# Attention and two MLPs from one written order: a new order table, with 185 copies, conversions and additions on other engines

## The chip, the cores and the metric

The kernel runs on one core of a Trainium2 chip. The metric is the device time of one execution in microseconds; the median of three executions of the kernel before is 849.13 us (848.77 to 849.22).

## The reference

Windowed attention (4 batches, 8 heads, 576 positions, 64 per head; heads 0 to 3 look back over 32 positions, heads 4 to 7 over 32 positions that lie four apart) and behind it two MLPs with 2304 tokens, 512 model columns and 2048 hidden columns:

```python
scores = np.where(masks[None], scale * np.matmul(q, k.transpose(0, 1, 3, 2)), -1e9)
attn = np.exp(scores - np.max(scores, axis=-1, keepdims=True))
attn = attn / (np.sum(attn, axis=-1, keepdims=True) + 1e-09)
x = np.matmul(attn, v)                        # heads side by side: 2304 x 512
h = x @ moe_w_in;  r = np.maximum(h, 0.0);  x = (r * r) @ moe_w_out
h = x @ moe2_w_in; return (h * (1.0 / (1.0 + np.exp(-h)))) @ moe2_w_out
```

## The kernel before, in words

**Tiling.** The attention goes by half a batch (`h` = 0 to 7) and pair of heads (`pair` = 0 to 3), in units of 96 or 72 queries: scores on TensorE (L533), mask and minimum on VectorE (L558), exponential on ScalarE (L566, or L729 behind a transposition for the first eight blocks), the sum and its reciprocal on VectorE (L573, L575, L744, L746), normalisation (L586, L590, L592, L754), transposition (L602, L713) and the product with V (L625, L738). The first MLP takes its first three tiles of 256 tokens while the attention still runs (`mlp`, L788 to L790 and L836 to L838) and its last three tiles of 512 tokens by a product that saves one multiplication in eight (`mlp2`, L936 and L990 to L992). The second MLP takes three tiles of 768 tokens in the same saving form for both of its products (`strassen`, L1094 and L1179).

**Number format.** Every operand of a large product is split in a high part (a conversion, L245 on ScalarE, L247 on VectorE, L249 on GpSimd) and a low part (a subtraction, L252 on VectorE or GpSimd), and each product is three matmuls. The weights come as 64-bit numbers and are turned into such pairs by nine small operations (`weights`, L274 to L330); later tiles read the pairs, and sums of them, back from HBM (`stream`, L445, and `stream2`, L472).

**What sets the order.** Nothing is scheduled while the kernel is built. Each operation has a number, and the table `ORDER` (from line 1359) lists all 3960 of them with the engine that does each: P is TensorE, A is ScalarE, V is VectorE, G is GpSimd, D is a DMA. `@` gives the place of its buffers or banks. Every engine does its words in the table's order and waits, at the head of its queue, for what the word needs. All DMAs, loads and stores alike, stand in one queue, that of SyncE: a word that waits for its buffer holds all DMAs behind it. A load can start once the operation that last read its place is done. `F14` is not an operation of the program but 14 matmuls on zeros (`filler`, L1245), put where TensorE would otherwise sit still.

```python
            o.eng = {"P": "PE", "A": "ACT", "V": "DVE", "G": "Pool", "D": "DMA"}[word[0]]
...
            elif o.eng == "Pool":
                o.turn = turn
```

The second of these places makes a GpSimd operation wait for the last VectorE operation before it in the table that is marked with `lock`.

**Words that the prediction names.** `D2`, `D33`, `D64` and `D95` load Q and K of pairs 0 to 3 of the first half (L495), `D3`, `D34`, `D65` and `D96` their V; `P5`, `P36` and `P67` are the scores of pairs 0 to 2 (L533), `P10` the first transposition (L713), `P13` the first product with V (L738). `D126` and `D135` load the first weights (L274), `A136` is the first step of their conversion (L282). `A3958` is a one-column exponential that stands first on ScalarE (L1304). `D3196` loads a pair of weight sums for the second product of the second MLP (L472), `P3438` is the product that reads it (L1179); `D758`, `D998` and `D1091` load blocks of later halves (L486), and `P759`, `P999` and `P1092` are their scores.

Of the kernel before, what the change touches and what calls it, by code (L numbers as in the profile page):

```python
# [1363 lines left out]
V110 D152@56 P86@2 V76 V103 A137 V77 V112 P104@1 A78@8 V113 V87 F7@3 V97 V114 V88 A105 V130 D177@88 A89 P115@1
V139 P106@0 A116 V131 F1@2 P90@3 D169@80 P117@2 V140 A91@60 A93@64 A132@68 F5@1 V94 V92 A141@164 V107 V118
P400@3@1@72@0 V108 V119 D211@124 G133 A153@14 V109@12 V120 A162 V403 F2@2 V401 A145 P121@0 G142 V402 V410
D506@201 P404@2 V411 A122 A144@10 V123 V412 A154 V146 P1238@3 D186@92 V399 A161@2 V147 A170@0 V148 P413@1 A124
A405 V178@4 D220@128 A149@84 V125 V163 A1239@16 P406@0 V150 A414 A1240 V164 P415@2 A179 D194@108 V407 V155
P1244@3 A1241@6 V408 V165 A409@8 V416 V156 A166@100 D424@196 P507@0@1@96@1 V417 V1242 A418 V157 P1243 A1245@18
V167 A158@168 D151 V172 A1246 V510 A187@10 D134 P419@3 V159 P1250@2 A422@104 A420 V512 A1247@12 G189 V508 V423  # L1370
A513 V421 A171 D203@116 V1248 P426@3@0@112@2 V180 A1251@16 V173 A511 P1249 A509 V427 G174 V523 A1252 V428 A188
V429 V436 V438 A1253@14 P430@2 V525 A524 V437 V514 V521 A526 V515 V425 V1254 A522 P439@1 V190 A431 A516 V527
A517 V175@172 P432@3 V528 V176 A440 A529 P518@0 V530 A222 P441@2 V433 V181 A204@2 P531@1 P1255 V434 V442 A520
V182 A435@8 V443 V519 A533 V444 D539@196 A532 A183@120 V191 P534@3 A195@6 V184 P445@0 A537@12 A535 V446 P1256@1
A192@176 G197 V448 V536 A196 V447 D450@201 V449 V198 A205 V193 A1257@18 P540@0@3@20@3 A1258 V199 A1259@4 D237@40
A212@0 V1260 V554 A200@28 P1261 V556 G206 V545 A557 V558 V543 A555 D254@76 V541 V201 A559 P452@0@3@24@0 A542
V560 V207 A544 A546 V561 D538 V451 P1262@1 V208 D271@112 A562 A563 V547 V465 V548 V455 A549 V466 G550 V454
P564@2 V463 A1263@16 D228@36 V464 A565 V456 A1264 V453 A566 V209@180 P551@1 A1265@8 V214 P457@2 A552 A553 V210
A221@14 D245@72 P567@1 V215 A458 A213 V223 P467@0 V1266 A238@12 V216 P459@3 A568 A468 V224 D572@196 A570@4
A217@32 P469@2 V240 A229@10 V225 P1267 A256 V460 V470 V461 V471 G218 V462@6 A239 D478@201 V472 A246@8 V569  # L1380
P473@0 V231 P1274@1 A476@52 A474 V241 A230 V475 A226@184 D262@92 V477 V232 P573@3@0@56@1 A1275@18 V227 A1276
A1277@2 V233 D296@116 A255@6 P480@1@2@80@2 V589 V587 A234@88 G1278 V580 V593 V576 A590 V574 G235 V591 P1279 A247
V483 D305@24 V484 V482 A592 V481 V493 A575 V492 V494 A581 P485@0 V578 V491 A577 D202 V248 A588 V263@10 P495@3
A579 V242 A486 A594 V582 P1286@0 A243@188 V583 D279@108 V479 V595 V584 A272@0 V596 V249 P585@1 V597 A1287@16
P487@2 D219 V244 A586 A496 P598@1 V250 A1288 D571 P497@3 D288@124 A599 V488 A1289@2 V489 P600@0 A490@14 V498
V1290 V499 V251@96 P1291 V257 A500 V252 D605@201 A603@4 V265 P501@2 V258 P1298@1 A504 A502 V601 A280@8 D638@196
V503 V505 V274 P1268@3 V602 A1299@18 V275 A1300 D322@56 A264 V259 P606@2@1@20@3 A273 V266 A1301@12 P1280@0
A1269@16 D604 V611 G281 D313@80 V609 V626 A1270 V620 V624 A610 V607 V267 A625 P1292@3 A1271@2 V613 A260@192 V622
V1302 A290 V261 P1304@2 A1281@18 V282 A612 V1272 A621 V268@128 A1293@16 V276 P639@1@36@0 A1294 A614 V269 A623
P640@3 A627 A1282 V628 V641 P1273 A608 V645 A1283@14 V615 V652 V629 G1284 V616 V654 A630 V643 V656 P1303 V289@2  # L1390
# [12 lines left out]
P1358@2 A722 A328@140 V1350 V1575@14 P1364@3 V1356 A1359@16 V329 D1573 A1360 A331@4 V1576@24 V1578@84 P1370@2
A1361@0 V1577 A1365@18 V1569 D693 A1366 A1580 D356@108 V1362 P727@3@80@3 V1579 A1371@16 V343 A1583 P1351 A1372
V733 D1570 V731 V729 V735 V344 A736 P723@2 A734 V1584 A345@148 P728@3 V333 A730 V1581 A1367@10 P1357 A732 V1368
A724@6 V742 D758@196 A332 V746 V737 V748 V744 V357@14 P1382@2 A745 V738 A749 V739 D1585 A743 V334 A747 P740@3
A1383@18 V358 P1363 A741 V335 A1373@2 D364@36 A1384 V750 A336@116 V751 V359 P759@3@2@76@0 V1374 A1385@8 V337
A752 D321 P1369 V773 V762 D725 V760 A348@0 V775 V764 D1582 A761 V1386 P1376@3 V350 A763 V349 A765 V777 A774 V766
# [265 lines left out]
```

## Time and profile before

| | before |
|---|---|
| median of three executions | 849.13 us |
| the profiled execution, whole | 849.5 us |
| its span, first to last instruction | 847.7 us |
[...]
| TensorE busy | 839.2 us (99%) |
| VectorE busy | 638.8 us (75%) |
| ScalarE busy | 501.5 us (59%) |
| GpSimd busy | 122.2 us (14%) |
| moved by DMA | 223.56 MB |

The span is one execution from its first instruction to its last; 1.8 us of the execution's time lie outside it. The shares are means over the whole span, and the stages differ much: ScalarE and VectorE have most of their work in the first 200 us. TensorE's busy time holds the 53 filler matmuls too.

### The profile page before, as it was taken

To read this page: it belongs to the slowest core of one execution; us is meant where nothing else is said; L and a number is where in the kernel's file an instruction comes from. 1 tells how busy PE (TensorE), PEld (TensorE's weight loads), DVE (VectorE), ACT (ScalarE), POOL (GpSimd) and SP (SyncE) were. 2 spreads that over 40 slices of the span, in tenths; PEclk is the share of its full clock that TensorE was granted. 3 is DMA by queue.
4 is the path that set the end of the run, shared out by engine and by line. 5 is a ranking of instruction groups with operands and counts; after the bars stand their busy time and mean duration, and the time that the engine had idled before them with its cause. 6 is when DMAs were issued, how large, how long until landed. Compare 5 with 4: busy or idle time off the path is not lost.

```text
span 847.7 us, 16967 instructions
## 1 busy us (share of the span) xinstructions
PE 839.2 (99%) x6009; PEld 795.6 (94%) x6009; DVE 638.8 (75%) x1706; ACT 501.5 (59%) x1324; POOL 122.2 (14%) x142
## 2 busy tenths in 40 slices
PE   9989999999999999999999999999999999999998
PEld 7879999999989889889998999999999999999998
DVE  6999999888888698768899997578722488422765
ACT  5999988887666265334542566565445555345652
POOL 2220000101210202131201002102201111202020
PEclk9999999999999999999999999999999999999999
DMA  9585568879898888988999989889774774773441
GB/s 344 178 284 207 152 204 304 278 265 333 310 303 318 308 292 282 326 311 288 336 344 299 343 308 351 301 287 324 248 259 149 246 266 164 269 262 111 174 159 65
DMA packets 83603, 223.56 MB, mean 264 GB/s; under 512 B 8768, under 2 KB 18240, under 8 KB 83520
## 3 DMA queue, kind: packets, MB, share of 16 engines
q1 hardware_dynamic: 83520, 222.49, 75.2%
q8 instruction: 47, 0.77, 0.3%
q14 instruction: 36, 0.29, 0.1%
HBM read 172.13 MB, written 50.33 MB: 262 GB/s over the span
## 4 chain that ended last, share of the span: by engine, by line
PE 94%; ACT 3%; DVE 1%; issue 0%; POOL 0%; POOLq 0%; ACTq 0%
PE y L1094 17%; PE sa L1179 15%; PE s L936 15%; PE y L1179 6%; PE y L990 5%; PE y L991 5%; PE y L992 5%; PE sa L1094 4%; PE s L788 3%; PE s L789 2%; PE s L790 2%; PE ax L533 2%; PE y L836 2%; PE ax L625 2%; PE y L837 2%; PE y L838 2%
## 5 line engine op out<-in xcount | busy, mean ns | idle before, releaser
L245 ACT CAST hl<-gq 128x384 fp32r<-128x384 f32 x168 | 79.5, 513 | 58.7 <-PE sa L1179 28.6
L1094 PE MATMUL y<-xs,ws 128*128 128x384 f32 x552 | 107.5, 334 | 0.0
L252 DVE TENSOR_TENSOR hl<-gq,hl 128x384 fp32r<-128x384 f32 x144 | 78.9, 581 | 27.3 <-ACT hl L245 24.0
L1094 PEld LDWEIGHTS y<-xs,ws 128*128 128x128 f32 x552 | 96.6, 188 | 0.1
L1065 DVE TENSOR_TENSOR gq<-y,gq 128x384 f32<-128x384 f32 x46 | 25.0, 554 | 94.1 <-PE y L1094 82.9
L1070 ACT COPY gq<-y 128x384 f32<-128x384 f32 x92 | 42.7, 479 | 75.0 <-PE y L1094 67.6
L1179 PE MATMUL sa<-hl,wp 128*128 128x384 f32 x432 | 79.1, 334 | 0.0
L936 PE MATMUL s<-x,ws 128*128 128x256 f32 x576 | 76.2, 284 | 0.0
L990 PE MATMUL y<-g,w 128*128 128x512 f32 x192 | 76.2, 397 | 0.0
L1179 PEld LDWEIGHTS sa<-hl,wp 128*128 128x128 f32 x432 | 75.2, 188 | 0.0
L991 PE MATMUL y<-g,w 128*128 128x512 f32 x192 | 75.2, 392 | 0.0
L992 PE MATMUL y<-g,w 128*128 128x512 f32 x192 | 74.9, 390 | 0.0
L952 DVE TENSOR_TENSOR h<-s,h 128x512 f32<-128x512 f32 x96 | 59.4, 619 | 19.8 <-PE s L936 16.6
L936 PEld LDWEIGHTS s<-x,ws 128*128 128x128 f32 x576 | 72.2, 191 | 1.2
L245 ACT CAST g<-r 128x256 fp32r<-128x256 f32 (+1 forms) x86 | 42.9, 504 | 51.2 <-DVE r L972 42.8
L566 ACT ACTIVATE ap<-ap,ast 96x128 f32<-96x128 f32 (+3 forms) x168 | 62.2, 371 | 8.3 <-DVE ast L575 4.2
L788 PE MATMUL s<-x,w 128*128 128x256 f32 x192 | 56.4, 294 | 0.1
L790 PE MATMUL s<-x,w 128*128 128x256 f32 x192 | 54.3, 283 | 0.0
L789 PE MATMUL s<-x,w 128*128 128x256 f32 x192 | 54.2, 282 | 0.0
L1179 PE MATMUL y<-hl,sw 128*128 128x384 f32 x288 | 51.4, 334 | 0.0
L1179 PE MATMUL sa<-hl,sw 128*128 128x384 f32 x288 | 50.9, 334 | 0.0
L1179 PEld LDWEIGHTS y<-hl,sw 128*128 128x128 f32 x288 | 50.0, 188 | 0.0
(176 smaller groups left out, 2071.2 us busy)
## 6 DMA issues: line engine op xcount, KB each, us to landing
raw<-w SPq DMA_DIRECT2D x64, 512.0 KB, 6.3
ws<-w1x SPq DMA_DIRECT2D x48, 512.0 KB, 6.7
ws<-w2x SPq DMA_DIRECT2D x48, 512.0 KB, 5.4
sw<-w2y SPq DMA_DIRECT2D x48, 512.0 KB, 4.5
wa<-w1s SPq DMA_DIRECT2D x24, 512.0 KB, 6.8
wa<-w2s SPq DMA_DIRECT2D x24, 512.0 KB, 5.7
w1x<-st SPq DMA_DIRECT2D x16, 512.0 KB, 4.8
w2x<-st SPq DMA_DIRECT2D x16, 512.0 KB, 5.1
```

The source lines that it names most:

```text
L245: self.nc.scalar.copy(out=out, in_=in_)
L252: self.eng[eng].tensor_tensor(out=out, in0=a, in1=b, op=ALU.subtract)
L566: es.append(self.op({"ACT": c_act(nk) + 0.185}, lambda e, i=i, n=n, c=c, p=p, st=st: nc.scalar.activation(out=p.tile[:n, c], in_=p.tile[:n ...
L788: nc.tensor.matmul(o, wh.tile[:, s], xh, start=(kk == 0), stop=False)
L789: nc.tensor.matmul(o, wh.tile[:, s], xl, start=False, stop=False)
L790: nc.tensor.matmul(o, wl.tile[:, s], xh, start=False, stop=(kk == KC - 1))
L936: nc.tensor.matmul(bank.tile[:, o:o + 256], wp, xp, start=i == 0, stop=last, skip_group_check=True)
L990: nc.tensor.matmul(o, wh.tile[:, s], gh.tile, start=c == 0, stop=False)
L991: nc.tensor.matmul(o, wh.tile[:, s], gl.tile, start=False, stop=False)
L992: nc.tensor.matmul(o, wl.tile[:, s], gh.tile, start=False, stop=(c == NF - 1))
L1094: nc.tensor.matmul(o, w[part == 2].tile[:, kk * P:kk * P + P], x[b][part == 1].tile[:, kk * half:kk * half + half], start=new and not kk a ...
L1179: nc.tensor.matmul(o, u.tile[:, c * P:c * P + P], v.tile, start=new and not q and not part, stop=q == nf - 1 and part == 2, skip_group_che ...
```

## The change

Only `ORDER` changes. The operations, their arithmetic and the code that makes them are the same. Counted from the two tables:

- 185 operations change their engine: 81 from ScalarE to VectorE, 47 from VectorE to ScalarE, 47 from GpSimd to VectorE, 10 from GpSimd to ScalarE. VectorE has 1560 words in place of 1479, ScalarE 1068 in place of 1092, GpSimd 66 in place of 123. TensorE has the same 750 and SyncE the same 516.
- By TensorE's place in the table before: in the first 24 us 3 go from ScalarE to VectorE and 1 from GpSimd to VectorE (the two subtractions of `V20`, L691). To 64 us 3 go from ScalarE to VectorE and 4 back. From 64 to 190 us 32 go from ScalarE to VectorE, 15 back, 3 from GpSimd to VectorE and 1 from GpSimd to ScalarE. The other 123 lie behind 190 us: among them 43 from GpSimd to VectorE.
- The fillers are 47 matmuls in eight groups (10, 16, 2, 7, 4, 2, 3, 3) in place of 53 in nine.
- The first loads are in another order: before `D3 D2 D33 D64 D126 D34 D135 D65 D95 D96`, after `D2 D33 D64 D135 D95 D96 D3 D65 D34 D126`. `P36` stands ahead of the second group of fillers, not behind it.
- `A3958` stands behind 19 other words of ScalarE, the first of which is `A136`.
- Other transfers change their turn and their buffers. Counted in words of TensorE between the one that frees the place (or holds the queue) and the one that reads the load: `D3196` has 4 in place of 8, `D758`, `D998` and `D1091` have 4 in place of 5. The load of weight sums next in shortness, `D3592`, has 5 in place of 22. No other load that TensorE reads directly, behind the first 30 us, comes below 6 us by the durations of TensorE's words before.

```diff
 ORDER = """
-V1 A3958 G0 F14@0 D3@140 D2@132 D33@136 V4 D64@144 D126@24 P5@20@0 F15@2 V8 V7 D34@148 V6 V18 D135@32 V9 V19
-P10@3 P36@28@1 V17 V50 P67@36@2 G20 A12 V38 A11 V49 V37 D65@156 V48 P13@0 V39 V68 V40 D95@152 P21@1 F3@3 V51 A22
...
-V3416 P3409 V3420 A3433@119 D3195@100 A3389 G3434 P3413 A3436@131 V3137 D3196@96 P3417 G3431 P3421 A3442@128
...
+V1 F10@3 D2@146 P5@44@0 G0 V7 V19 V8 V17 V6 D33@172 P36@163@1 V9 V18 V37 V50 V49 V39 V48 V20 V38 V40 D64@11
+F16@3 D135@201 V51 A136@32 V138 V137 P10@3 A11 D95@20 A12 D96@131 V97 D3@100 D65@55 V4 P67@40@2 V79 V80 V68 V82
+V70 V71 P21@3 A22 A23 P41@2 A43 P52@0 A53 V81 D34@89 V35 A42 D126@176 P13@1 V14 V15 V69 V66 A54 P24@3 V25 V72
...
+V3468 A3469@3 V3476 V3446 V3428 V3498 V3480 V3504 D3197@186 V3456 D3194@104 P3426 D3195@99 P3429 P3432 D3196@120
+P3435 P3438 P3441 A3457@128 V3458 A3461@58 V3454 V3536 D3132@16 P3444 P3447 D3133 D3198@22 A3423 A3509@74
...
 """
```

## Rows read from the trace of the kernel before

**Rows 1.** The page, part 1: busy time, share and instructions of each engine.
```profile
span 847.7 us, 16967 instructions
PE 839.2 (99%) x6009; PEld 795.6 (94%) x6009; DVE 638.8 (75%) x1706; ACT 501.5 (59%) x1324; POOL 122.2 (14%) x142
```

**Rows 2.** Busy time by stretch: length, then PE, PEld, DVE, ACT, POOL, clock, DMA.
```profile
0.00:21.00 21.00, 19.43 (x199) 15.76 (x200) 13.24 (x93) 11.08 (x41) 4.95 (x15) 1.00 0.92 343
21.00:63.00 42.00, 38.65 (x388) 34.64 (x387) 41.09 (x179) 41.26 (x123) 9.06 (x11) 1.00 0.68 231
63.00:191.00 128.00, 127.86 (x1214) 122.50 (x1213) 119.26 (x406) 112.39 (x372) 5.40 (x8) 1.00 0.69 235
191.00:480.00 289.00, 289.00 (x2133) 261.33 (x2132) 243.00 (x615) 143.19 (x409) 48.35 (x61) 1.00 0.90 314
480.00:848.00 368.00, 364.22 (x2084) 361.33 (x2082) 222.16 (x418) 193.61 (x384) 54.40 (x48) 1.00 0.67 233
```

**Rows 3.** Waits of PE over the whole span: total, times, longest, in us.
```profile
PE y L837 <- POOL g L252: 0.9, 1, 0.9
PE y L836 <- ACT g L245: 0.8, 1, 0.8
PE ax L738 <- DVE x L252: 0.5, 1, 0.5
```

**Rows 4.** Timeline of the first 12 us: start, length, instruction, idle time before it.
```profile
0.72 1.28 ACT L1304 ACT_TABLE_LOAD   x1 [0.72 <-PEq L1665]
...
0.98 3.17 PE L1245 MATMUL fill<-warm 128*128 128x256 bf16 x14 [0.98 <-DVE warm L1237]
...
4.09 1.49 PE L533 MATMUL y<-w 64*96 64x96 f32 x12
...
5.51 2.52 PE L1245 MATMUL fill<-warm 128*128 128x256 bf16 x15
5.72 0.29 DVE L558 CUSTOM_DVE_ANT_0 ap<-y,mask 96x128 f32<-96x128 f32 x1 [2.39 <-PE y L533]
...
9.11 0.29 DVE L558 CUSTOM_DVE_ANT_0 ap<-y,mask 96x128 f32<-96x128 f32 x1 [1.60 <-PE y L533]
```

**Rows 5.** Groups of instructions: one conversion on ACT and on DVE.
```profile
L245 ACT CAST w<-cv 128x512 fp32r<-128x512 f32 x27 | 16.6, 619 | 0.7 <-DVE cv L318 0.7
...
L247 DVE CAST w<-cv 128x512 fp32r<-128x512 f32 x5 | 2.1, 414 | 0.0
```

**Rows 6.** Timeline near 800 us: DVE alone, DVE in a row, DVE beside POOL.
```profile
800.08 0.55 DVE L252 TENSOR_TENSOR gq<-gq 128x384 f32<-128x384 f32 x1
800.55 1.49 DVE L252 TENSOR_TENSOR hl<-gq,hl 128x384 fp32r<-128x384 f32 x3
...
803.63 2.71 DVE L252 TENSOR_TENSOR hl<-gq,hl 128x384 fp32r<-128x384 f32 x3 [0.66 <-ACT hl L245]
...
804.65 1.26 POOL L252 TENSOR_TENSOR gq<-gq 128x384 f32<-128x384 f32 x1 [0.49 <-DVE hl L252]
```

**Rows 7.** Waits of DVE between 63 and 191 us: the three longest, all on ACT.
```profile
DVE ast L573 <- ACT ap L566: 1.9, 7, 0.5
DVE g L252 <- ACT g L245: 1.3, 4, 0.4
DVE st L252 <- ACT st L245: 1.2, 2, 0.7
```

**Rows 8.** The chain, one group of six matmuls of the second MLP.
```profile
523.85 1.04 PE sa L1179 x6
```

**Rows 9.** DMA issues: count, KB each, median us from issue to landing.
```profile
sw<-w2y SPq DMA_DIRECT2D x48, 512.0 KB, 4.5
...
blk<-qkv SPq DMA_DIRECT2D x6, 544.0 KB, 3.7
...
blk<-qkv SPq DMA_DIRECT2D x6, 480.0 KB, 4.3
```

**Rows 10.** All loads of the weight sums (tile sw).
```profile
DMA to landing us min/median/max: 3.5/4.5/9.9
```

More of the change, by code (lines that the diff above doesn't have):

```diff
@@ L1364 @@
[L1364 to L1378, printed above, removed]
@@ L1404 @@
[L1404 to L1408, printed above, removed]
@@ new lines @@
+V26 P44@2 V83 V45 V46 P98@77@3 V110 A16@25 A27 D398@196 D177@121 A47@171 P55@0 P73@3 A74 P28@1 V100 V101 F2@2
+V56 V113 V57 V99 V58 P59@2 A29@44 A60 P84@3 A85 V102 V112 V30 P75@0 V31@48 A62 G127@169 G129 A128 V103 P104@3
+A105 A3958 V32 V76 V63 V61 P86@2 V77 V111 V114 A78@163 F7@1 V87 V88 A89 F4@1 P115@0 A116 V139 V130 P90@3 A93@64
+A91@60 V140 V131 A132@68 G133 A141@164 D152@158 D186@185 D143@8 A145 G142 P106@0 V107 V92 V94 V108 P117@2 V118
+V109@25 D160@101 D506@115 V119 V120 A153@98 P400@3@1@79@0 V403 F2@0 V411 V410 P121@0 F3@2 V412 V402 V401 A124
@@ new lines @@
+A331@155 V320 V333 P1346@2 A1347@80 A1348 D356@108 A1568 V1576@24 V326 V327 P1339 A1571 A720 P708@2 A709 P691@3
+A692@0 P1345 V1569 A340@9 V342 A1355@13 V343 V344 P721@3 A1349@157 A722 A328@140 P1358@2 A1359@151 A1360
+A1361@76 P1364@3 A1365@21 A1366 A1367@162 V332 V1356 V334 V1350 D236 V1577 V1368 P1370@2 A1371@3 A1372 A1373@160
+D726@201 V1578@84 V1572 P727@3@80@2 V731 V1579 A1583 V735 A736 V729 A732 V733 A734 V1362 V1584 P1351 P728@3
+V1374 P723@2 V748 A749 V329 D168 D693 V744 D347@112 D321 D1570 D758@196 D1573 P1357 A730 A724@15 D725 A745 V742
@@ new lines @@
+P937@3@2@56@2 D1711@30 D2132@128 V942 V953 A954 V2165 P1525 A1544@10 A1542@46 V951 V940 A941 V957 V955 A958
+V1546@120 V1548@13 A943 A952 A956 A1538@3 P2166 V938 V959 V960 A939 P2174@2 A2178@16 V944 A945 D1543
+P968@0@1@68@3 V986 V971 A972 A1704 G1705 V973 V961 P2167 V969 V975 V946 V947 A948 P2168 P2169 P962@3 V963 V1706
+V982 A974 P2175@2 V2179 G1699 V1700 P949@0 D2129@38 D935 P2176@3 A950 P964@2 D1539 D2130@96 D998@201 A983 A970
+V988 V984 D1701 A976 V977 V978 G979 A987 V1713 A985 V2180 V2181 A989 V1707 A1708@43 P2177@1 V990 V2182 V991
@@ new lines @@
+D2135@70 D2138@8 P2211@1 V2216 V1728 V2217@98 D1091@196 D1719 P1092@2@0@68@3 V1095 V1112 A1087 V1097 V1108 V1106
+P1088@3 A1089@128 V1110 V1099 V2221@47 V1093 D2141@0 D2145@56 D2139@38 D2151@130 D1028 D2144@23 D1059 D2142@32
+D1739@92 D2148@64 P2225@1 P2226@3 A1113 A1100 P2227@0 P2228@2 A1107 A1111 A2218@17 A2229@8 V2219 V2230 V2231
+P2220 V2232 A2222@51 V2223 A1094 V2233 P2224 A1098 A1096 V1101 V2238@21 A1109 V1114 V1102 A1103 D1090 D2146@80
+P1104@0 A1105 P2242@2 V1115 V1116 V1741 A2246@96 P1117@1 A1118 D2149@37 D1729 D2150@116 D2152@16 P2243@3 V1740@2
@@ new lines @@
+V2457 P2445 D2357@20 D2530@56 P2482@0 P2483@2 A2473@60 G1826 A1825 A2484@40 V2320@110 V2474 P2458 V2485
+A2321@104 V2322 A1871@6 V1872 D2531@18 D2533@64 D1822 G1873 A2324@36 V2486 V1827 V1828 V1874 V1875 A2477@196
+V2478 A1829@108 A1811 V1832@32 V2325 P2462 P2475 P2562@1 G1834@128 V1833 G1835 V2487 V2488 V2489@202 A2312@52
+A2310@76 A2318@112 V2493@81 A2494@88 V2311 V2313 V1830 A2490@10 A1839 V2319 D2532@116 P2563@2 P2564@3 D1878@124
+A1880 V1879@84 V1881 V1882 A1836 V1837 A2566@20 V2567 P2479 V2568 V1883 V2495 V2569 V1886@124 V2491 V1840
@@ new lines @@
+D3154@39 D3067 P3107 P3111 V3118 A2726@55 V3122 V3028 V3094 V2730 D3065 P3202 V2722 A2724@15 P3115 P3119
+D3156@35 P3204 P3206@0 V2725 V2727 G2731 A3203@52 P3208 A3205@61 A3209 P3123 P3210 A2732@28 V2733 V3211
+D3160@125 D3158@104 P3212 D3029 D3169@42 D3166@130 D3162@48 D3171@40 D3175@12 D3164@99 P3214 A3215@71 P3127
+P3216 P3219@3 D3183@180 V3217 A3213@68 V3220 P3221 P3223 A3222 A3218 D3163@4 P3226 V3227 A3224 V3207 A3225 P3228
+A3229@81 P3230 P3232 V3233 P3235@0 P3237 P3239 A3231@84 A3238 A3240 D3176@64 D3165@35 P3242 D3168@120 D3093
@@ new lines @@
+V3482 V3520 P3483 P3490@1@2 P3493 P3496 P3499 P3502 P3505 V3507 P3508 A3521@126 A3517@96 V3518 V3448 G3526
+D3568@100 V3137 V3138 D3565@14 V3540 A3139@55 A3541@47 V3484 A3529@51 V3486 D3485 D3561@132 D3487 D3555@4
+D3569@72 A3141@87 V3522 P3511 P3600 V3512 D3581@2 D3556@80 D3554@10 P3519 P3523 V3140 V3143 V3142 V3530 V3542
+A3144@34 V3148 V3145 A3146@74 V3151 A3149@40 V3150 V3147 V3514 P3527 P3531 P3535 P3539 D3573@119 D3576@174
+D3558@150 D3562@122 D3451 P3543 P3547 A3548@127 P3602 A3550 A3601@16 A3603@19 P3604@1 A3152@46 D3559@95 P3606
@@ new lines @@
+A3664 D3574@8 P3674 P3676 P3678 P3681@3 A3648 V3673 A3675@151 P3683 A3671 V3679 V3762 A3677@161 A3684 P3685
+A3686 P3688 V3689 D3578@12 D3582@127 D3579@96 P3690 P3692 P3694 V3695 V3682 V3666 A3737@114 A3691@68 A3693@71
+V3738 P3697@1 P3699 P3701 A3763@65 A3702 P3704 A3731@131 D3580@100 P3706 P3708 A3700 D3577@0 A3703 A3687
+A3707@22 V3732 V3753 A3754@119 P3710 V3766 V3755 V3698 V3711 P3713@0 P3715 P3717 G3729 P3730@1@2 A3743@124
+A3740@86 G3741 A3680 G3770 A3709@25 A3716 A3767@9 V3792 V3764 A3718 V3744 A3696 V3774 A3775@128 V3796 A3797@13
@@ new lines @@
+A3817@120 A3843@123 V3896 V3832 V3794 P3781 P3785 D3591@186 D3588@89 P3791 P3795 D3589@132 P3799 D3590@96
+A3889@101 A3786@126 A3787 V3835 V3844 V3854 V3866 A3809@4 V3838 A3855@176 A3892@90 V3887 V3814 V3810 V3899 V3856
+V3818 P3803 P3807 P3811 P3815 V3862 A3863@74 P3819 D3592@12 D3593@104 V3823 P3824 P3827 V3890 V3870 V3878 V3850
+A3851@119 V3864 V3914 D3595@86 D3594@130 P3830 A3867@65 A3840@41 V3852 V3893 V3841 V3918 A3904@187 V3905
+A3907@45 V3908 D3596@4 A3915@116 A3859@36 P3833 P3836 P3839 P3842 V3902 V3922 V3874 V3930 A3931@129 V3868 P3845
@@ new lines @@
+A3820@32 A3871@12 A3821 A3919@105 V3860 V3942 D3597@48 V3920 V3872 G3938 D3598@133 P3853 P3857 P3861 P3865 P3869
+P3873 A3943@5 A3939@113 A3879@8 V3848 V3880 V3932 A3923@19 A3875@87 V3876 V3924 D3599@41 P3877 P3881 V3846 V3934
+V3882 V3916 V3884 D3885 V3940 P3888@0@3 P3891 P3894 P3897 V3926 P3900 P3903 P3906 P3909 D3847 P3917 P3921
+A3927@48 V3910 V3928 P3925 P3929 P3933 V3944 A3935@174 V3936 P3937 P3941 P3945 P3948 A3946@81 P3949 P3950 V3912
+P3951 P3952 P3953 D3911 P3954 P3955 D3883 D3947 D3913 D3849 A3956 D3957
```

418 lines of the change are left out of this document (193 added, 225 removed).

## The prediction, made before the change was run

> **What bounds the kernel now.** I read the page's busy times first, then busy time by stretch, then TensorE's waits, then the first 12 us of the timeline.
>
> The page says that TensorE is busy for 839.2 of 847.7 us [rows 1]. So all that another order can win back is the rest, 8.5 us, and the fillers among the busy time. The stretches say where the rest lies [rows 2]: 1.57 us in the first 21 us, 3.35 us from 21 to 63 us, 0.14 us from 63 to 191, nothing from 191 to 480, and 3.78 us behind 480. The last is mainly the end: the final copy and store, which both tables have alike. So only the first 63 us hold a gain, about 4.9 us of idle time plus the fillers. Two groups of fillers there, of 14 and 15, take 3.17 and 2.52 us [rows 4]; they stand where TensorE has nothing to do, so taking a filler out wins nothing by itself.
>
> From 21 to 63 us VectorE is busy for 41.09 of 42 us (97.8%) and ScalarE for 41.26: both are full, and TensorE's waits there are for them, 0.5 to 0.9 us each [rows 2, 3]. From 63 to 191 us VectorE is busy for 119.26 of 128 us and ScalarE for 112.39, while TensorE hardly waits. That is the reserve of the stage: 8.7 us on VectorE, 15.6 us on ScalarE. Behind 191 us VectorE and ScalarE have room (46 us in the next 289, 146 in the last 368).
>
> **The change part by part.** *The start.* The scores of the first pair begin at 4.09 us, and VectorE's first minimum at 5.72 us, behind a wait of 2.39 us; at 9.11 us it waits 1.60 us more, for the second pair's scores, which stand behind the 15 fillers and the first transposition [rows 4]. After the change the Q and K of the pairs are loaded first, without V of pair 0 ahead of them, and `P36` stands ahead of its fillers. Ten fillers in place of 14, at 3.17/14 = 0.23 us each, end 0.9 us earlier, at 3.2 us. I put the gain at 0.7 us, because the Q and K block still has to land, plus the 1.60 us of the second wait: 2.3 us. Against it stand four operations more on VectorE before 24 us: three at 0.34 us (below) and the two subtractions of `V20`, about 0.5 us together, 1.5 us in all. V of pair 0 comes seventh and not first; `P13` waits for it, and what then runs in its place is the next pairs' work. Net: 0.8 us won. Bounds: 2.3 us won if the added work lies in VectorE's other waits, and 1.3 us lost (the table load below).
>
> *21 to 63 us.* Three operations go to VectorE and four leave it: nothing.
>
> *63 to 191 us.* Net 32 + 3 - 15 = 20 operations come to VectorE. A conversion takes 0.414 us there and 0.619 us on ScalarE [rows 5]. Neighbours on VectorE overlap: three of 0.55 us in a row take 1.49 us, so each but the first costs 0.47, 0.08 us less [rows 6]. At 0.414 - 0.07 = 0.344 us, 20 of them add 6.9 us: 119.3 + 6.9 = 126.2 us of work on VectorE in a stage of 128 us. ScalarE gives up 16 net, at 0.5 to 0.6 us some 8 us, and then has over 20 us of room. This trade is the centre of the change: it unloads the engine that has the larger reserve. If VectorE can be kept as full as it is from 21 to 63 us, 97.8%, the stage takes 126.2/0.978 = 129.0 us: 1.0 us lost. Bounds: nothing lost, if its remaining waits fit into 1.8 us; 6.9 us lost, if all 8.7 us of its idle time come again. I take 1.0, because the three longest of those waits, 4.4 us together, are for ScalarE [rows 7], and ScalarE is what gets lighter.
>
> [...] Beside one GpSimd addition of 1.26 us, three VectorE instructions took 2.71 us, where three alone took 1.49 [rows 6]: 1.2 us lost on VectorE. [...]
>
> *Behind 191 us.* 43 GpSimd operations go to VectorE, 0.5 us each, some 20 us; 46 and 146 us of room cover them, and TensorE stood still nowhere there. If that cover were gone in one place, the price is one late operand, 0.5 to 0.9 us as in [rows 3].
>
> *The transfers.* All stand in one queue, so I counted for every load how many words of TensorE lie between its release and its use. `D3196` falls from eight groups to four, of 1.04 us each [rows 8]: 4.2 us, where loads of its kind need 3.5 at least, 4.5 in the median and 9.9 at most [rows 10]. That makes 0.3 us of waiting, bounds nothing and 5.7 us. `D3592` has five groups, 5.2 us. `D758`, `D998` and `D1091` keep 4.8 to 4.9 us where their kinds land in 4.3 and 3.7 us [rows 9]: nothing, up to 1 us each if another load is ahead. I take 0.3 us for all.
>
> *The table load.* It runs now at 0.72 us, beside the first fillers, for 1.28 us [rows 4]. With `A3958` moved behind `A136`, it may run only ahead of the first exponential of the attention, at about 8 us; price 0 to 1.28 us, taken as 0, because V of pair 0, now late, holds `P13` at that time anyway. [...]
>
> **Sum:** -0.8 + 0 + 1.0 + 0 + 0.3 = +0.5 us. The profiled execution took 849.5 us, 0.4 us above the median of the three; from it 850.0, and against the median 849.6 us. A measurement of this kernel can tell about 0.2% (1.7 us) from no change, so I forecast **no difference that can be measured**.
>
> **The rivals.** *VectorE becomes the bound (slower).* Place: 63 to 191 us. What speaks for it: 126.2 us of work in 128 us, in an engine that takes its words strictly in order; and from 21 to 63 us, where VectorE and ScalarE are both full, TensorE lost 3.35 of 42 us [rows 2]. Against it: ScalarE is light then. If all 8.7 us of idle time come again, the stage takes 6.9 us more: 849.1 - 0.8 + 6.9 + 0.3 = 855.5 us. The forecast allows 2.8 us of idle time (129.0 - 126.2); slower by over 0.2% begins where 1.2 us more, some 4 us, come again.
>
> *The start wins more (faster).* VectorE begins 2.3 us earlier, the added work fits into waits, and the middle loses nothing since GpSimd holds VectorE up less: 849.1 - 2.3 = 846.8 us. For it: the two waits of 4.0 us together [rows 4] are real and their causes are moved. Against it: from 21 to 63 us both other engines stay full, so what is gained early has to pass through them.
>
> *The table load comes late (slower).* 1.28 us on ScalarE's first chain: 849.6 + 1.3 = 850.9 us, on the edge of what can be told.
>
> *The change doesn't do what it says:* it can't be, the table is the program's only order.
>
> **How the numbers follow.** No measurable difference 0.44, with its own range of 847.6 to 850.8 us; VectorE as the bound 0.34; a faster start 0.17; the late table load 0.05, which I count as slower. So faster 0.17, same 0.44, slower 0.39. The range runs from 847.0 us (half of the faster case) to 854.0 us (most of the slower one, up to some 5.4 us of loss in the middle).
>
> **What would show it.** Right: VectorE's first minimum near 5 us and no wait of 1.6 us near 9; VectorE busy for 97 to 98% from 63 to 191 us, ScalarE below 83%; TensorE's idle time there 0.5 to 2 us; no wait of TensorE on a DMA above 0.5 us but ahead of `P3438`. Wrong: VectorE below 95% with TensorE waiting on it (the slower rival), TensorE's idle time in the first 63 us below 3 us (the faster one), a table load between 7 and 10 us, or a wait on a load of over 1 us, which would mean that the count of words between release and use is no measure of a load's margin.

## The result, and the profile after

The change makes the kernel slower: 859.12 us in the median (857.05 to 859.43) against 849.08 us, a ratio of 1.0114 with a 95% interval of 1.0096 to 1.0131. The forecast was no difference that can be measured, 849.6 us, in a range of 847.0 to 854.0 us. Neither the forecast nor the slower rival (855.5 us) reached so far.

Part 1 of the page of the changed kernel, against [rows 1]:

```profile
span 857.5 us, 16888 instructions
PE 840.7 (98%) x6003; PEld 797.2 (93%) x6003; DVE 671.8 (78%) x1788; ACT 486.8 (57%) x1295; POOL 75.8 (9%) x79
```

Its busy times by the stretches of [rows 2] (columns: stretch, length, busy time of PE, PEld, DVE, ACT and POOL with the instructions, granted clock as a share of full speed, DMA share, GB/s):

```profile
0.00:21.00 21.00, 17.63 (x189) 14.25 (x189) 15.26 (x99) 11.28 (x40) 2.96 (x12) 1.00 0.91 335
21.00:63.00 42.00, 39.12 (x396) 35.30 (x397) 41.16 (x178) 40.23 (x122) 9.76 (x11) 1.00 0.76 258
63.00:191.00 128.00, 127.69 (x1214) 122.70 (x1213) 124.75 (x425) 105.14 (x350) 2.27 (x3) 1.00 0.67 224
191.00:480.00 289.00, 283.08 (x2073) 256.37 (x2073) 242.01 (x628) 132.94 (x394) 30.93 (x32) 0.99 0.84 299
480.00:857.50 377.50, 373.14 (x2136) 368.62 (x2135) 248.66 (x464) 197.24 (x393) 29.88 (x22) 1.00 0.67 240
```

The stage from 63 to 191 us is close to the forecast: VectorE is busy for 124.75 of 128 us (97.5%), ScalarE for 82%, and TensorE is idle for 0.31 us, under the 0.5 to 2 us that the prediction names. The new hole is in the row below it. Before, TensorE had no idle time from 191 to 480 us [rows 2]; now it has 5.9 us, and the mean clock is 0.99 (over the whole span 0.996 of full speed, 0.999 before).

To put the loss in place I matched TensorE's words in the two traces and added up how much longer each now takes until the next one begins (fillers are counted too; the stretches are those of the changed kernel):

```
0 to 21 us     -0.50       375 to 390 us  +1.39
21 to 63       -0.22       390 to 540     +0.27
63 to 192.6    +0.04       540 to 570     +0.67
192.6 to 215   +7.28       570 to the end +0.02
215 to 375     +0.19       sum            +9.14
```

The last 0.7 us of the two spans' difference (9.8 us) lies behind TensorE's last instruction, in the final copy and store. So the first 63 us win 0.7 us, the middle costs nothing, and 7.3 of the 10 us are lost in one place of some 20 us. The waits of TensorE behind 191 us name what it waited for there:

```profile
engine line waited for: us in total, times, longest us
PE y L836 <- DVE yo L247: 3.2, 1, 3.2
PE s L936 <- DMA ws<-w1x: 1.3, 1, 1.3
PE y L836 <- ACT yo L245: 1.2, 1, 1.2
PE y L1094 <- DMA ws<-w2x: 0.2, 1, 0.2
```

**The stop.** `yo` are the copies of the first MLP's finished output from PSUM (`mlp`, L849). Four of them, `A1526`, `A1528`, `V1530` and `A1532`, empty the first token tile's halves of four banks; each can begin once `P1435` has ended. The next tile uses the other halves of the same banks. In the kernel before, `V1530` and `P1465`, the next tile's product that writes those banks behind it, began so (start, duration, engine, line, operation, and in brackets the idle time before it and its releaser):

```profile
186.62 0.42 DVE L247 COPY yo<-y 128x256 f32<-128x256 f32 x1 [0.65 <-PE y L838]
...
188.22 0.28 PE L836 MATMUL y<-g,w 128*128 128x256 f32 x1
```

The timeline of the changed kernel around the stop:

```profile
186.22 0.37 ACT L245 COPY yo<-y 128x256 f32<-128x256 f32 x1
...
191.87 0.90 PE L533 MATMUL ax<-blk 64*96 64x128 f32 x12
...
192.69 0.38 PE L836 MATMUL y<-g,w 128*128 128x256 f32 x1
...
192.95 0.28 DVE L558 CUSTOM_DVE_ANT_0 ap<-ax,mask 96x128 f32<-96x128 f32 x1
...
193.39 0.28 PE L838 MATMUL y<-g,w 128*128 128x256 f32 x1
...
194.68 0.28 DVE L558 CUSTOM_DVE_ANT_0 ap<-ax,mask 96x128 f32<-96x128 f32 x1
...
195.82 0.68 DVE L903 TENSOR_TENSOR stg<-xr,stg 128x512 f32<-128x512 f32 x1
...
196.42 0.41 DVE L247 COPY yo<-y 128x256 f32<-128x256 f32 x1
...
196.89 0.58 PE L836 MATMUL y<-g,w 128*128 128x256 f32 x1 [3.22 <-DVE yo L247]
...
197.27 0.41 PE L837 MATMUL y<-g,w 128*128 128x256 f32 x1
```

At 191.87 us TensorE computes `P883`, the scores of an attention pair, and at 192.69 us begins `P1465`. Six of its 12 matmuls run; the seventh writes the bank that `V1530` has still to read. `V1530` could have begun at 186.2 us, when `P1435` ended. But in the new table it stands behind the six minima of `P883` (L558), two subtractions (L252), two steps of a weight's conversion (L284, L302) and `V2091` (L903), all of them words that VectorE does in their order. So VectorE is never idle, and TensorE waits for the end of twelve of its words, `V1530` the last of them; the first could not start before TensorE itself had done `P883`. It began at 192.95 us, 0.2 us behind the end of `P883`, so less work on VectorE ahead of it could have won no more than these 0.2 us. Before the change `V1530` ran 1.60 us ahead of `P1465`. This kernel guards PSUM by bank: the halves that are read and written are different ones, and the wait of 3.22 us is there. Whether the copy or the product waits is set by the table: `A1526`, the copy of the first bank, stands behind `P1465` in it, and `P1465`'s first three matmuls, which write the other half of that bank, began at 192.69 us although `A1526` read its half at 208.25.

The second stop, 1.22 us ahead of `P1489`, has the same form:

```profile
208.25 0.37 ACT L245 COPY yo<-y 128x256 f32<-128x256 f32 x1
...
208.76 0.35 PE L836 MATMUL y<-g,w 128*128 128x256 f32 x1 [1.22 <-ACT yo L245]
```

`A1526` stands on ScalarE behind `A1680`, which converts a weight and waited until 207.65 us for VectorE's `V1679`.

**The clock.** The same stretch, one microsecond a row:

```profile
193.00:194.00 1.00, 0.67 (x6) 0.47 (x4) 1.00 (x10) 1.00 (x4) 0.73 (x2) 1.00 0.80 117
...
195.00:196.00 1.00, 0.00 (x0) 0.00 (x0) 1.00 (x3) 1.00 (x6) 0.00 (x0) 0.88 1.00 388
196.00:197.00 1.00, 0.11 (x1) 0.11 (x1) 1.00 (x3) 0.60 (x4) 0.00 (x0) 0.50 1.09 409
...
202.00:203.00 1.00, 1.00 (x8) 1.00 (x8) 0.00 (x0) 0.00 (x0) 0.00 (x0) 0.71 0.73 256
203.00:204.00 1.00, 1.00 (x10) 1.00 (x10) 0.00 (x0) 0.69 (x2) 0.00 (x0) 1.00 0.24 80
```

About 2 us into the stop, in the row that begins at 195 us, the granted clock falls from 1.00 to 0.50 of full speed, and it comes back in the row that begins at 202 us, after some 5.7 us of work at half speed (that row's 0.71 puts it near 202.6 us). I put the rest of the 7.28 us down to it: 3.22 + 1.22 us of stops leave 2.84 us, half of those 5.7. TensorE reads as fully busy there; only the clock column and the matmuls' 0.41 us in place of 0.28 show it.

**The start** went as forecast in most points:

```profile
0.73 1.28 ACT L282 ACT_TABLE_LOAD   x1 [0.73 <-PEq L1665]
...
5.06 0.29 DVE L558 CUSTOM_DVE_ANT_0 ap<-y,mask 96x128 f32<-96x128 f32 x1 [4.13 <-PE y L533]
...
8.40 0.66 ACT L282 ACTIVATE cv<-raw 128x512 f32<-128x512 f32 x1 [6.39 <-DMA raw<-w]
8.96 0.45 ACT L729 ACTIVATE ap<-ax 96x96 f32<-96x96 f32 x2
...
9.46 0.96 PE L713 MATMUL ax<-ident,ap 96*128 96x96 f32 x9 [0.88 <-ACT ap L729]
```

VectorE's first minimum is at 5.06 us (5.72 before [rows 4]), and the wait of 1.60 us near 9 us is gone. But `A136` (L282) waits until 8.40 us for its load, and the first exponential (L729) stands behind it: TensorE waits 0.88 us for that.

### The profile page after: what moved, and what is told of

It reads as the page before. It is cut to its first block, busy times and chain, and to the rows that moved or that the text cites. A ratio compares the mean times of both kernels' runs of the same rounds, so it can differ in the third digit from the quotient of the medians.

```text
span 857.5 us, 16888 instructions
## 1 busy us (share of the span) xinstructions
PE 840.7 (98%) x6003; PEld 797.2 (93%) x6003; DVE 671.8 (78%) x1788; ACT 486.8 (57%) x1295; POOL 75.8 (9%) x79
## 4 chain that ended last, share of the span: by engine, by line
PE 72%; DMA 2%; issue 0%; ACT 0%; DVE 0%; ACTq 0%
PE y L1094 16%; PE sa L1179 14%; PE s L936 13%; PE y L1179 6%; PE y L990 5%; PE y L991 5%; PE y L992 5%; PE sa L1094 4%; PE ax L533 1%; DMA ws<-w2x 1%; PE ax L625 1%; DMA ws<-w1x 1%; PE ax L602 1%; DMA blk<-qkv 1%; PE zx L836 0%
## 5 line engine op out<-in xcount | busy, mean ns | idle before, releaser
L252 DVE TENSOR_TENSOR hl<-gq,hl 128x384 fp32r<-128x384 f32 x154 | 83.5, 579 | 26.1 <-ACT hl L245 26.0
L1065 DVE TENSOR_TENSOR gq<-y,gq 128x384 f32<-128x384 f32 x46 | 25.3, 554 | 65.8 <-PE y L1094 44.6
L952 DVE TENSOR_TENSOR h<-s,h 128x512 f32<-128x512 f32 (+1 forms) x96 | 59.4, 620 | 19.5 <-PE s L936 13.5
L252 DVE TENSOR_TENSOR gq<-gq 128x384 f32<-128x384 f32 x92 | 51.9, 584 | 1.7 <-ACT gq L1130 1.4
L252 DVE TENSOR_TENSOR g<-r,g 128x256 fp32r<-128x256 f32 (+1 forms) x89 | 49.1, 558 | 5.0 <-ACT g L245 3.2
```

The source lines that it names most:

```text
L252: self.eng[eng].tensor_tensor(out=out, in0=a, in1=b, op=ALU.subtract)
L952: add = lambda o, a, b: nc.vector.tensor_tensor(out=o, in0=a, in1=b, op=ALU.add)
```

## The experiments

In each diff the words shown are those of the table; a word with `-` leaves its place for the one with `+`.

**One copy early.**

```diff
 A1643 P1435
+V1530@46
 A1532@13 A1468
...
 V1677 V2091@110
-V1530@46
 D1531 D1533
```

> The changed kernel with one word of the table moved: V1530, the copy of the third output bank of the first token tile, stands directly behind P1435, as in the kernel before, and not behind the row minima of the pair P883. Theory A (one late copy): TensorE stops 3.22 us in the middle of P1465 only because V1530 stands behind minima that wait for P883, which TensorE computes directly ahead of P1465; the half clock behind it is its consequence. Then the stop of 3.2 us and the stretch at 1.2 GHz (3.0 us more for P1465 to P1496 than at full clock) both go, the second stop of 1.2 us ahead of P1489 stays: some 6 us less than the changed kernel, 853 us. Rival B (VectorE is the bound from 63 to 191 us and its debt falls due here): the work on VectorE is the same, so another result of it comes late and TensorE's idle time from 191 to 212 us stays at about 4 us: 858 to 859 us.

Measured: 851.79 us (851.23 to 852.10), ratio 1.0027 (1.0017 to 1.0037). TensorE's waits from 180 to 215 us:

```profile
PE y L836 <- ACT yo L245: 1.2, 1, 1.2
```

The first stop and the half clock are gone (1.00 in the mean from 191 to 215 us, 0.86 in the changed kernel), the second stop is left, as theory A has it. No run shows a clock in GHz: what the expectation calls 1.2 GHz is measured as 0.50 of full speed. One word, on the same engine and at the same ring place, gives back 7.3 of the 10 us: by TensorE's words 6.0 at the stop and 1.4 near 379 us, where the stop for a load did not come in this execution. With these 1.4 us it would be the expected 853 us. Nothing else became late, although VectorE has the same work: rival B falls.

**Both copies early.** As above, and:

```diff
 V1530@46 A1532@13
+A1526@80
 A1468 P1484@3
...
 D1531
+D1527
 D1533 A2089@100
...
 V1679 A1680@80
-A1526@9
 P1489 A1534@93
...
 V913 A914
-D1527
 D2122@96 D1682
```

> As evict_one, and A1526, the copy of the first bank, moved in the same way (directly behind A1532, at ring place 80, its store D1527 directly behind D1531). Theory A: the second stop of 1.2 us goes too; in all 7.2 us less than the changed kernel: 852 us; what is left against the kernel before is a stop for a load near 379 us and some smaller losses, less the 0.7 us won at the start. Rival B: 858 to 859 us, with TensorE idle for about 4 us somewhere between 191 and 215 us.

Measured: 849.79 us (849.36 to 850.52), ratio 1.0008 (0.9999 to 1.0018): no difference from the kernel before. It is 2.2 us less than expected, since the stop near 379 us did not come here either and less was lost near 555 us. The middle and the stage behind it:

```profile
63.00:191.00 128.00, 127.71 (x1214) 122.72 (x1214) 125.35 (x427) 105.25 (x350) 2.28 (x3) 1.00 0.67 224
191.00:215.00 24.00, 24.00 (x225) 23.06 (x223) 22.15 (x72) 17.65 (x56) 6.38 (x3) 1.00 0.90 318
```

VectorE is as full as in the changed kernel, and TensorE loses nothing. So the places of the two copies are the cause of the loss at 192 to 215 us, and the 97.5% on VectorE are not.

**A copy made late in the kernel before.** The mirror, in the old table (`V1660` and `V1470` stood between already):

```diff
 D1654 P1478@2
-V1530@12
 A1526@14 A1528@10 V1660 A1473@18 V1470
-P1465
 V1676 A1479@16 V2088@8 D1527 A1640 D1529 V1641 A2089@100
-D1531 P1471 D2081
 A1474 V1666@80 A1661@20 V1644
-D882@201
 A1475@14 V1664@128
+V1480 V1662 V1530@12 P1465 P1471 D2081 D882@201
 P1484@3 A1532@0
-V1480 V1662
+D1531
```

> The kernel before with V1530 and P1465 behind eleven more words of VectorE (V1676, V2088, V1641, V1666, V1644, V1664, V1480, V1662 with the ScalarE words that they need); all engines, all places and every other order as before, but the store D1531 behind D882. V1530 then ends about 3.5 us later, near 192 us, and P1465 stops for 2 to 3 us at its seventh to tenth multiplication. Theory A: 2 to 3 us of stop and about as much again by the half clock: 4 to 6 us slower than before, 853 to 855 us. Rival B (one late copy in a stage where VectorE has room is caught up with): 849 to 850 us.

Measured: 854.15 us (854.01 to 857.40), ratio 1.0063 (1.0044 to 1.0082). The longest wait of TensorE, and the clock behind it:

```profile
PE y L836 <- DVE yo L247: 3.5, 1, 3.5
```

```profile
193.00:194.00 1.00, 0.00 (x0) 0.00 (x0) 1.00 (x3) 0.00 (x0) 0.00 (x0) 0.91 0.58 234
194.00:195.00 1.00, 0.74 (x3) 0.74 (x4) 0.54 (x2) 0.00 (x0) 0.00 (x0) 0.50 0.01 4
...
198.00:199.00 1.00, 1.00 (x10) 1.00 (x10) 0.96 (x3) 0.00 (x0) 0.00 (x0) 1.00 0.58 226
```

By the words of TensorE, `P1465` and `P1471` take 5.1 us more: 3.5 of stop, 1.6 left for the half clock, as theory A has it. It is not caught up with: from 200 us on TensorE's words win nothing of it back. (The profiled execution is the one of 857.40 us; it lost 1.8 us more in its first 63 us.)

**The copy half as late.**

```diff
 V1494 V899
+V1530@46
 V1672 D1673 V1677 V2091@110
-V1530@46
 D1531 D1533
```

> The changed kernel with V1530 three words earlier, ahead of V1672, V1677 and V2091, still behind the minima of P883. By the timeline of the changed kernel V1530 then ends near 195.3 us, and TensorE stops for about 1.7 us in place of 3.2. Theory A (stop and half clock are two prices): a stop of 1.7 us leaves the clock at 1.0, as the stops of 2.1 to 2.3 us in the filler runs did while they lasted; 1.5 us less stop and 2.8 us less half clock: 4.3 us less than the changed kernel, 854.8 us, or 853.5 where the load near 379 us is in time. Rival (each us of a late copy costs the same): 1.5/3.2 of 5.9 us less: 856.4 us.

Measured: 853.73 us (852.98 to 855.15), ratio 1.0058 (1.0045 to 1.0071). The stop is 1.53 us, and the clock holds at 1.00:

```profile
PE y L836 <- DVE yo L247: 1.5, 1, 1.5
```

```profile
195.00:197.00 2.00, 1.89 (x15) 1.89 (x16) 2.00 (x6) 1.32 (x8) 0.00 (x0) 1.00 1.05 397
197.00:199.00 2.00, 2.00 (x19) 2.00 (x18) 1.55 (x4) 0.00 (x0) 0.00 (x0) 1.00 1.04 389
```

Three words of VectorE, 1.7 us of stop, are worth 5.4 us of time. By TensorE's words 4.2 us lie between 192 and 215 us, 1.7 of stop and 2.5 that went with the half clock; 0.7 lie near 379 us, where the stop for the load was 0.5 us in place of 1.3; and 0.5 near 555 us. The rival, by which each us of a late copy costs the same, falls: it had 856.4 us.

**Fillers in the stop.** 27, then 6 of them, between `P883` and `P1465`:

```diff
 V2083 V901
+F27@2
 P1465 P1477
```

> The changed kernel with 27 filler multiplications (3.2 us at full clock, by 0.12 us each) between P883 and P1465. V1530 comes as late as before, so P1465 gets no earlier; TensorE only stays busy while it waits. Theory A1 (the half clock costs as much as the stop, and comes from it): the granted clock stays at 1.0 and P1465 to P1496 run at full speed: 2.7 us less than the changed kernel, 856.4 us. Rival A2 (these multiplications are slow for another reason, or the idle time of 1.2 us ahead of P1489 takes up what is won): no change, 859 us, or worse if the fillers themselves delay P1465.

> As fill_wait, with 6 fillers (0.7 us) in place of 27. In fill_wait the bank of the fillers came free only 2.27 us after P883, so they ran too late and held P1465 up by about 2.4 us beyond V1530; six of them, from 2.27 us on, end in time for P1465's first nine multiplications (1.0 us) to be done when V1530 is. So the start of its tenth stays as in the changed kernel, and no single idle stretch is over 2.3 us. Theory A1 (the half clock costs 2.7 us of the 7.2 lost from 192 to 212 us): the clock stays at 1.0 and TensorE stands, at 215 us, 2.7 us ahead of the changed kernel; 856 us, or 855 where the load near 379 us is in time as in the other runs. Rival A2 (P1465 to P1496 run slowly for another reason): TensorE at 215 us as in the changed kernel.

Measured: 856.61 us (856.15 to 858.07), ratio 1.0086 (1.0071 to 1.0101), with 27; 855.78 us (854.52 to 856.87), ratio 1.0078 (1.0065 to 1.0091), with six. The times are as expected, but that is luck: in the profiled executions TensorE won 0.8 us from 190 to 215 us with 27 fillers and 1.5 with six, not the 2.7 of the expectation, and the rest came from the stop near 379 us, which did not come in either (1.6), and from near 555 us (0.5). The fillers' bank came free late, so TensorE was idle for over 2 us in both, 2.27 us with 27 and 2.11 with six. With 27 the clock stayed at 1.00 and the fillers' length was lost in its place. With six the clock still fell, about a microsecond after TensorE had begun to work again, and for a shorter time (some 3.4 us in place of 6.8, estimated from the clock column's rows); the expectation that it would stay is a miss. (Six matmuls of `P1465` ran behind the fillers, not nine, as the expectation has it.)

```profile
194.84 0.81 PE L1245 MATMUL fill<-warm 128*128 128x256 bf16 x6 [2.11 <-DVE ast L558]
```

```profile
195.00:196.00 1.00, 1.00 (x11) 0.95 (x10) 1.00 (x3) 1.00 (x7) 1.00 (x1) 0.97 1.01 377
196.00:197.00 1.00, 0.89 (x5) 0.59 (x4) 1.00 (x4) 0.37 (x2) 0.78 (x1) 0.50 1.07 416
...
199.00:200.00 1.00, 1.00 (x9) 1.00 (x8) 0.00 (x0) 0.00 (x0) 0.00 (x0) 0.82 1.01 325
```

That the half speed comes from the stop, theory A1, is borne out by the 27 fillers and by the copies that were moved early: in those runs the same matmuls have the full clock, 1.00 in the mean from 191 to 215 us. Its price of 2.7 us is not measured cleanly here, since the clock fell with six and the fillers themselves cost time with 27. The better measure of it is the half-late copy, with 2.5 us.

**Engines without the order, and the order without the engines.** The 185 engine letters of the change in the old table; and the letters of the kernel before in the table with both copies early:

```diff
-G20
+V20
...
-A137
+V137
...
```

> The order, the places and the transfers of the kernel before, with the 185 moved operations on the engines of the change. My prediction's step: 6.9 us of work more on VectorE from 63 to 191 us cost between nothing and 6.9 us, taken as 1.0; behind 191 us nothing. Theory A (the engines are not the cause, the place of two copies in the order is): within 1.5 us of the kernel before, 848.5 to 850.7 us, VectorE busy for about 97% from 63 to 191 us and TensorE idle there for under 1 us. Rival B (the engines cost time, and the change's order only hides it): 852 us or more, with TensorE's waits for VectorE between 63 and 191 us.

> evict_two with the 185 operations back on the engines of the kernel before: the change's order alone. Theory A (the engines cost nothing, and win nothing behind 63 us): 849 to 851 us, as evict_two (849.8) within 1 us. Rival B (the engines cost the 0.5 us that evict_two has left over the kernel before, or more): 849 us or less. Rival C (the engines are what wins the 0.7 us of the first 63 us): about 850.5 us, with the loss in the first 63 us.

Measured: 862.85 us (862.76 to 864.56), ratio 1.0166 (1.0153 to 1.0179), and 891.51 us (890.43 to 898.25), ratio 1.0511 (1.0486 to 1.0535). In the first, theory A falls and rival B's price holds, though TensorE's waits are for ScalarE and GpSimd too; in the second none of the three theories comes near (its profiled execution is the one of 898.25 us). From 63 to 191 us (the new engines in the old order, then the old engines in the new one):

```profile
63.00:191.00 128.00, 123.10 (x1149) 115.71 (x1149) 118.67 (x423) 101.50 (x343) 3.39 (x4) 1.00 0.65 223
```

```profile
63.00:191.00 128.00, 117.69 (x1057) 109.95 (x1056) 106.25 (x378) 100.70 (x333) 8.35 (x10) 0.96 0.55 184
```

With the new engines in the old order TensorE loses 6.75 us there, in many waits of 0.4 to 0.8 us, and 2.2 and 2.5 us in two later places (250 to 300 and 480 to 540 us), while VectorE and ScalarE both have idle time. The longest wait of that run has the form of the two stops above, and here the copy is one of the 185:

```profile
PE y L1094 <- DVE yo L247: 2.2, 1, 2.2
```

Operation 2710 copies a finished bank out of PSUM. In the kernel before ScalarE began it at 500.01 us, and `P2794`, which writes the bank next, began at 500.81 without a wait. As `V2710`, at the same place of the old order, it began at 513.41 us and ended at 514.09, and `P2794` waited for it until 514.14 us. The change has it on VectorE too, but at 503.85 us, 5 us ahead of `P2794`. So the engines are not free, and the order alone is worth nothing: they fit each other. In this stage the changed table makes the move of 20 operations to VectorE cost 0.04 us, which in the old order costs 6.75.

**The loads, and `A136`.** In the changed kernel `D2352` earlier; on top of both copies early, `D2352` and `D2764` earlier; on the same, `A136` behind the first exponentials; and all three together (`best`):

```diff
 V2442@36 P2407
+D2352@56
 D1814@196 V1815@200
...
 A2467@92 D2306@28
-D2352@59
 D2307 D2355@108
```

```diff
 A2922@67 D2761@10
+D2764@79
 D1869 P2879@3
```

```diff
 D135@201 V51
-A136@32 V138 V137
 P10@3 A11
...
 A22 A23
+A136@32 V138 V137
 P41@2 A43
```

> The changed kernel with D2352 alone moved (ahead of D1814, at ring place 56). Theory: the stop of 1.3 us ahead of P2464 near 379 us belongs to the changed kernel whenever its copies are late, and D2352 is released too late by V2410: 857.7 us, 1.4 less than the changed kernel. Rival: the load's landing varies from execution to execution, and the stop is there in some only (the four executions shown took 857.05 to 859.43 us): the median falls by less than 1 us, and the range stays.

> evict_two with the two loads moved as in best (D2352 ahead of D1814 at place 56, D2764 ahead of D1869), and A136 left where the change has it. Theory: D2764 takes back the 0.4 to 0.7 us lost near 555 us: 849.3 us, no difference from the kernel before that can be measured; the miss of best (850.7 us, and four executions of 860 us) came from A136. Rival: the moved loads are what failed in best: 850.5 us or more.

> evict_two with A136, V138 and V137 behind A23, and no load moved. Theory: it is A136 that made best slower than evict_two: 850.5 to 851 us in the median, some executions near 860 us at a lower granted clock, and TensorE about 0.6 us later than evict_two at 21 us. Rival (the moved loads did it): 849.8 us or, by what the first exponentials gain, 849.0.

> evict_two with three words more moved: A136 (which waits for a raw weight block until 8.4 us and holds the exponential A11 behind it) with V138 and V137 behind A23; the load D2352 ahead of D1814 at ring place 56 (TensorE stopped 1.3 us for it in the changed kernel); the load D2764 ahead of the store D1869 (TensorE lost 0.4 to 0.7 us for it). Theory: A136 wins up to 0.9 us at the start, D2764 0.4 us, D2352 nothing beside evict_two, where that stop did not come: 848.5 us, 0.7 us below the kernel before at most. Rival: from 21 to 63 us VectorE and ScalarE are full, so what the start wins is lost again there: 849.4 us.

Measured: `load_early` 857.02 us (856.45 to 858.57), ratio 1.0097 (1.0084 to 1.0110); `loads_two` 850.60 us (849.35 to 851.10), ratio 1.0014 (1.0006 to 1.0023); `exp_first` 851.20 us (849.65 to 860.98), ratio 1.0055 (1.0026 to 1.0085); `best` 850.73 us (849.86 to 861.53), ratio 1.0058 (1.0024 to 1.0092).

`load_early` has no stop near 379 us, but neither had the runs with fillers or with early copies, and the half-late copy had 0.5 us, all with `D2352` where the change has it. So the stop is not fixed by the table alone, and what the move is worth by itself stays open. How long such a load takes there, in the changed kernel from 340 to 385 us:

```profile
DMA to landing us min/median/max: 4.2/7.1/7.7
```

`D2352` was issued at 372.00 us, as soon as `V2410` had freed its place, and landed at 379.69: 7.7 us, in a queue that issued eight transfers in 6.2 us. `P2464` was there at 378.39.

`loads_two` won nothing; its time is the rival's, though its interval overlaps with that of both copies early alone. TensorE stops for 1.00 us at 551.76 us ahead of a product that reads another load of the same queue, which landed at 552.62 us (550.63 with both copies early alone).

```profile
552.76 1.28 PE L1094 MATMUL y<-xs,wc 128*128 128x384 f32 x6 [1.00 <-DVE hl L252]
```

(The profile names a subtraction of VectorE as the releaser. But the word of VectorE that this product has to wait for is the addition that reads its bank, L1065, and that one had ended at 550.28 us; the load's landing is what fits.)

The long executions of `best`, four of twelve at 859.5 us and more, come from the move of `A136`: without the moved loads `exp_first` behaves in the same way, and none of the eleven executions of `loads_two` is long. Of the 12 executions of `exp_first` five took 858.7 to 861.0 us, at a mean clock of 0.985 or 0.986; the other seven took 849.65 to 851.84. (The ratios of these two take in the long executions and lie above those of the medians.) The profiled one is of the long kind:

```profile
12.00:15.00 3.00, 2.45 (x23) 2.23 (x24) 1.93 (x16) 2.13 (x9) 0.00 (x0) 0.56 1.03 416
...
33.00:36.00 3.00, 3.00 (x16) 3.00 (x16) 1.87 (x4) 1.20 (x3) 0.00 (x0) 0.50 0.01 3
36.00:40.00 4.00, 3.78 (x33) 3.31 (x31) 2.30 (x7) 3.08 (x10) 0.00 (x0) 0.97 0.12 44
```

TensorE stood still for 0.33 and 0.72 us ahead of 12.6 us, and then ran at a clock of 0.50 for over 20 us. The long executions take 9.0 us more than the others (859.43 against 850.39 us in the medians). `best` has a stop of 0.8 us at the same place, and its profiled execution kept its clock, 1.00 in the means to 21 us and from 21 to 63 us. What decides it is open.

No version beats both kernels; the change with both copies early is level with the kernel before.

## Why the prediction was wrong

**The start: the gains right, the sum in part luck.** Forecast -0.8 us, measured -0.5 in the first 21 us. The minimum near 5 us (0.66 us earlier) and the missing wait near 9 (1.60 us) came as named. But the 0.88 us that TensorE lost because `A136` holds the exponentials behind it stand in no term, and no run measures by itself the 1.5 us that I set against the gains for VectorE's four more operations.

**21 to 63 us: right.** Nothing was forecast, and -0.2 us came.

**63 to 191 us: the work nearly right, its cost less.** I forecast 126.2 us of work on VectorE, a share of 97.8% and 1.0 us of loss, with bounds of 0 to 6.9. It was 124.75 us of busy time in 128, 97.5%, and 0.04 us. Both ends of the bound were seen: the changed table pays nothing, and the same engines in the old order pay 6.75 us. That this is near the rival's 6.9 us is partly chance, since many of those waits are for ScalarE and GpSimd. What I missed is that engines and order can't be priced apart: the table is a schedule, and a sum of work says only whether a good order can exist.

I also misread [rows 6]. Beside the three subtractions of 2.71 us stood two additions of GpSimd, the one that I named and one that began earlier:

```profile
803.15 1.01 POOL L252 TENSOR_TENSOR hl<-gq,hl 128x384 fp32r<-128x384 f32 x1 [19.26 <-DVE hl L252]
```

So the 1.2 us lost are 0.6 for each of the two, not 1.2 for one, and the four operations that leave GpSimd from 63 to 191 us would give back some 2.4 us (an estimate from these rows). No term of the sum used it.

**Behind 191 us: the step that failed.** I costed it at nothing, since 46 us of room cover 43 operations, and at 0.5 to 0.9 us "if that cover were gone in one place". Two operands came late there, `V1530` by 3.22 and `A1526` by 1.22 us, and the first stop also cost 2.84 us of half clock, a price that I had nowhere: 7.3 us in all. It was not the room on the engines that was gone: neither of the two copies is one of the 185; they kept their engines and only changed their places. I followed the moved operations and each engine's sum of work, but not, for each PSUM bank, where its last reader stands against the product that writes the bank next, and which words of the same queue have to wait for TensorE between the two. That can be read from the tables alone: `V1530` went from behind `P1478` to behind `P883` and the minima that read it, with `P1465` next.

**Transfers: the mechanism right, the place and the size wrong.** Forecast 0.3 us, at `D3196`; measured no wait of 0.2 us or more there, 1.4 us at `D2352` and 0.7 us near 555 us, in the profiled execution. I set aside every load with a margin of over 6 us, against a median landing of 4.5 [rows 10]. But those rows are of the second product's weight sums. `D2352` is of another kind, and the page of the kernel before had its landing, in the median of 48 loads:

```profile
ws<-w1x SPq DMA_DIRECT2D x48, 512.0 KB, 6.7
```

`D2352` has 6.4 us and took 7.7. By the sign that the prediction names, the count of words is no measure of the margin unless the landing is that of the load's own kind and stretch; and the same margin held in most of the runs above, so the price is not a fixed one.

**The table load: right, at nothing, for another reason.** I had it run at about 8 us and cost nothing, because V of pair 0 comes late. It runs at 0.73 us, although the word behind it waits until 8.40. In the order of the queue it is what ScalarE does ahead of `A136`. But it did not wait for `A136`'s operand, and so its 1.28 us were over at 2.01 us, 6.39 us before `A136` began.

**The rivals.** VectorE as the bound had the right sign, but the wrong place and the wrong cause: the changed kernel reached 859 us with VectorE's work from 63 to 191 us at no cost, and with the two copies moved and VectorE as full the loss behind it was gone.

## What to carry to other kernels

When an order changes, go through the buffers and not only the operations that changed engines: for each PSUM bank or ring place that is used again, look at the last reader's place in its queue against the next writer, and ask whether a word in between waits for the writer's own engine. A stop of TensorE can cost more than its length: here stops of 3.2 to 3.5 us took 1.6 to 2.8 us more by the half clock behind them. Look for that in the clock column, where busy time shows nothing. Engine choices and order belong together; either half alone cost 14 and 42 us here.

## What the runs showed that was not expected

- Stops of 1.22 us (the change), 1.53 (the half-late copy) and 2.2 (the new engines in the old order) left the clock at 1.00; stops of 3.22 us (the change) and 3.53 (the mirror) were followed by 0.50. The half clock behind them cost 2.84 and 1.6 us, so its price varies even where the stop is nearly the same. Behind 2.11 us of idle time and six fillers the clock fell too; behind 2.27 us and 27 fillers it did not.
- In the attention's small products of the first 36 us TensorE stayed at a clock of 0.50 for over 20 us while, from 15 us on, 93 to 100% busy (`exp_first`). Five of twelve executions of that table and four of twelve of `best` were some 9 us longer at a lower mean clock (0.983 to 0.986); no execution shown of the kernel before or of the change was.
- Moving one load ahead in the single DMA queue was followed by a stop for another: 1.0 us at 551.76 us, where both copies early alone have none over 0.2 us.
